# Bias matmuls of batch 0 on four quarter tiles, and one transpose of batch 2 moved from DMA to PE, in a fused attention and token-mixing kernel

## The chip, the cores and the metric

The kernel runs on one core of one Trainium2 chip. The metric is the device time of one execution in microseconds, lower is better. A core has five engines with an instruction queue each: PE (TensorE, matrix products), DVE (VectorE), ACT (ScalarE), POOL (GpSimd) and SP (SyncE, here only an issuer of DMAs). Two on-chip memories matter: SBUF, 128 partitions wide, which all engines and the DMA engines reach, and PSUM, into which PE writes its products and from which DVE and ACT read. One PSUM bank holds 512 float32 numbers per partition.

## What is computed

Attention with a window and a few global keys, and then a token-mixing layer on its output, for 4 batches of 768 tokens, 8 heads of 64 channels:

```python
# attention; n_global = 8, n_local = 96
scores = scale * np.matmul(q, k.transpose(0, 1, 3, 2))
rel = pos[:, None] - pos[None, :]
is_global = pos[None, :] < int(n_global)
is_local = (rel >= 0) & (rel < int(n_local))
keep = is_global | is_local
dist = np.where(is_global & ~is_local, float(n_local), np.abs(rel))
slopes = 2.0 ** (-8.0 * (np.arange(H) + 1) / H)
scores = np.where(keep, scores - slopes[:, None, None] * dist, -1e9)
attn = softmax(scores) @ v                    # to x: 4 x 768 x 512
# mixing
theta = x @ w_theta
zr, zi = x * cos(theta), x * sin(theta)
u = x + w_tok_r @ zr + w_tok_i @ zi           # over tokens
out = u + relu(u @ w_ch)
```

The inputs are float32; the kernel casts them to bfloat16 on load and accumulates in float32.

## The kernel before, in words

**Tiles.** The 768 tokens are 6 tiles of 128 (`NT`), the 8 heads 4 pairs (`NP`); a pair's two heads lie in partitions 0 to 63 and 64 to 127 of `qT` and `kT` (channels in the partitions). Scores are made transposed, keys in the partitions, queries along the row: a key tile meets its own query tile and the next one, and through `kG`, a copy of a key tile whose first 8 keys are replaced by the global keys, the same matmul serves the window and the global keys. A *chunk* is two key tiles (`c` = 0, 1, 2), up to 4 blocks of 128 columns for each of two heads, one PSUM bank for each head: tile `pb`, 128 x 2 x 512. There are two such buffers.

**Biases.** The distances with their mask are a small table, `dist` (128 x 6 blocks x 128, `distances`, L121). In batches 1 to 3 the bias is multiplied in after the exponential, as a table `etab` (L322, L325 on DVE). In batch 0 it is added in PSUM by PE: `score_bias` (L278) multiplies a diagonal matrix `diag[:, h]`, which holds the head's slope, with the distances (L283, one matmul for each head, 512 columns, 384 in chunk 2), and `score_mms` (L287) accumulates the scores on it (L303, contraction over 64 channels in one half of the rows). `score_exp` (L309) is ACT's exponential (L313).

**Values and x.** `values` (L346) multiplies with v and a column of ones (L362); DVE takes the reciprocal (L371) and writes the normalized output to `x_sb` (L373). `vglob` (L335, L343 and L344 on DVE) makes `vG`, the v tiles with the global rows. `xtrans` (L375) turns a pair's part of x into `xT`, channels in the partitions: through a DMA transpose on SP (L377), or through six PE transposes against the identity (L384) into a small PSUM tile and a copy (L385). Batch 0 and pair 3 of batch 1 take the PE way, all others the DMA.

**Mixing.** `theta` (L390) multiplies `xT` with `w_theta` (L405), chunk by chunk of two token tiles; its first step leaves out the last quarter of the contraction, which is pair 3, and does it last. `sines` (L410) makes cos and sin on ACT (L415) and the products `zri` on DVE (L419). `mix` (L424) is the token mixing (L430), with `u` on DVE (L435); `utrans` (L439) turns `u`, by DMA (L444) or by PE (L448); `chan` (L451) is the last product (L458), the ReLU and sum on DVE (L463) and the output DMA on SP (L465). Small PSUM tiles (`ps`) come from a pool of four, in turn.

**Order.** Batch 0's attention and the start of its mixing are ordered by hand (L530 to L619), on all five queues. After that each batch's mixing is woven with the next batch's attention by weights (`weave`, L514, with the steps from `attention_steps`, L485), and a scheduler places what the queues run. POOL issues the loads, casting on the way (L73, L82, L88, L154, L158, L163): those of batch 0 and the weights at once, the rest as buffers come free. SP issues DMA transposes and outputs.

Of the kernel before, what the change touches and what calls it, by code (L numbers as in the profile page):

```python
# [10 lines left out]
BF = mybir.dt.bfloat16  # L11
# [5 lines left out]
def kernel(  # L17
# [13 lines left out]
    nc = tc.nc  # L31
    B, H, S, D = q.shape
    T = 128
# [3 lines left out]
    NP = H // 2  # L37
# [8 lines left out]
    const = ctx.enter_context(tc.tile_pool(name="const", bufs=1))  # L46
# [6 lines left out]
    def ps_big():  # L53
        return big.tile([T, 2, 512], FP, name="pb", tag="pb")

    def ps_small(shape, dtype):
        return small.tile(shape, dtype, name="ps", tag="ps")
# [40 lines left out]
    for i_, eng in ((1, nc.sync), (0, nc.scalar)):  # L98
        eng.dma_start(out=qk32[:, i_].rearrange("p h t d -> p h (t d)"),
                      in_=(q, k)[i_][0, 0:2].rearrange("h (p t) d -> p h (t d)", p=T))  # L100
# [17 lines left out]
    dist = const.tile([T, 6, T], BF)  # L118
    far = const.tile([T, 2 * T], FP)

    def distances():  # L121
        nc.vector.tensor_scalar(far, near, float(NL), 1e6, op0=ALU.is_ge, op1=ALU.mult)
        nc.vector.scalar_tensor_tensor(near, in0=near, scalar=-1e6, in1=near,
                                       op0=ALU.mult, op1=ALU.max)
        d2 = dist[:, 2:4].rearrange("p s n -> p (s n)")
        nc.vector.tensor_tensor(d2, near, far, op=ALU.max)
        nc.vector.memset(dist[0:NG, 3], float(NL))
        nc.vector.tensor_copy(out=dist[:, 0:2], in_=dist[:, 2:4])
        nc.vector.tensor_copy(out=dist[:, 4:6], in_=dist[:, 2:4])
        nc.vector.tensor_scalar(dist[0:NG, 0], dist[0:NG, 2], float(NL), None, op0=ALU.min)  # L130

    diag = const.tile([T, H, T], BF)

    def diagonals(p):
        for h in (2 * p, 2 * p + 1):
            nc.vector.tensor_scalar(diag[:, h], ident, -slopes[h] / scale, None, op0=ALU.mult)
# [41 lines left out]
    def warm(n):  # L178
        ps = ps_small([T, 512], FP)
        for _ in range(n):  # L180
            nc.tensor.matmul(ps, lhsT=zero[:, 0:T], rhs=zero, start=True, stop=True)
# [96 lines left out]
    def score_bias(p, c):  # L278
        pb = pbs[0, p, c] = ps_big()
        n = min(4, 2 * NT - 1 - 4 * c)  # L280
        s0 = 2 if c else 0
        for hh in range(2):
            nc.tensor.matmul(pb[:, hh, 0:n * T], lhsT=diag[:, 2 * p + hh],  # L283
                             rhs=dist[:, s0:s0 + n].rearrange("p s n -> p (s n)"),
                             start=True, stop=False)

    def score_mms(b, p, c):  # L287
        qT, kT, kG = qkT[(b, p)]
# [84 lines left out]
        nc.vector.tensor_mul(xv, po4[:, :, :, 0:D], rec.to_broadcast([T, n, nt, D]))  # L373

    def xtrans(b, p, copy=nc.vector.tensor_copy, i0=0, i1=NT):  # L375
        if b > 1 or (b and p < 3):
            anchor["sp"] = nc.sync.dma_start_transpose(  # L377
                out=xT_sb[b][:, p, :].rearrange("p (t s) -> p t s", t=NT),
                in_=x_sb[b][:, p].rearrange("p t d -> p (t d)")).ins
            return  # L380
        ps = ps_small([T, S], BF)
        own = slice(i0 * T, i1 * T)
        for st in range(i0, i1):
            nc.tensor.transpose(ps[:, st * T:(st + 1) * T], x_sb[b][:, p, st, :], ident)  # L384
        copy(out=xT_sb[b][:, p, own], in_=ps[:, own])  # L385
# [99 lines left out]
    def attention_steps(b, preps):  # L485

        steps = []
        add = lambda w, f, *a: steps.append((w, lambda: f(*a)))
        add(0, alloc_x, b)
        late = [lambda p=p: prep(2, p) for p in range(NP // 2, NP)] if b == 2 else []  # L490
        chunks = [(p, c) for p in range(NP) for c in range(NT // 2)]
        ahead = [preps[:1], preps[1:2], preps[2:]] if preps else [[]] * 3
        if b == B - 1:
            add(0, kglob, b, 0)
        for i_ in range(0, len(chunks), 2):
            steps.append((1800, lambda i_=i_: [scores(b, *pc) for pc in chunks[i_:i_ + 2]]))
            if i_ == 0:
                add(0, vglob, b, 0, H)
            if b == B - 1 and i_ in (0, 2, 6):
                add(0, kglob, b, (1, 2, 0, 3)[i_ // 2])  # L500
            if i_ in (0, 2):
                steps.extend((1536, f) for f in late[i_ // 2:i_ // 2 + 1])
            if i_ == 8:
                steps.extend((1536, f) for f in ahead[0])
            for p in [p for p in range(NP) if (i_ // 2, p) in ((2, 0), (3, 1), (5, 2))]:
                add(1600, lambda p=p: [values(b, p, 0), values(b, p, 1)])
                add(800, xtrans, b, p, nc.scalar.copy)
        steps.extend((1536, f) for f in ahead[1])
        add(1600, lambda: [values(b, NP - 1, 0), values(b, NP - 1, 1)])
        add(800, xtrans, b, NP - 1, nc.scalar.copy)  # L510
        steps.extend((1536, f) for f in ahead[2])
        return steps
# [21 lines left out]
    dve, act = nc.vector.tensor_copy, nc.scalar.copy  # L534
    warm(6)
    distances()
    diagonals(0)
    score_bias(0, 0)
    score_bias(0, 1)
    cast0(1, dve, 0)  # L540
    bias_table(0)
# [19 lines left out]
    for p in range(NP - 1):  # L561
        score_exp(0, p, 1)
        out0(p + 1, 1, act)
        out0(p + 1, 0, dve)
        kglob(0, p + 1)
        score_bias(p, 2)
        score_mms(0, p, 2)
        if p:
            values(0, p - 1, 0)
            values(0, p - 1, 1)  # L570
        score_exp(0, p, 2)
        if p < 2:
            vglob(0, 4 * p, 4)
        score_bias(p + 1, 0)
        score_mms(0, p + 1, 0)
        if p + 2 < NP:
            turn0(p + 2, 1)
            turn0(p + 2, 0)
        score_exp(0, p + 1, 0)
        score_bias(p + 1, 1)  # L580
        score_mms(0, p + 1, 1)
        if p == 1:
            xtrans(0, 0)
    p = NP - 1
# [121 lines left out]
```

## Time and profile before

| what | value |
|---|---|
| median of 4 runs | 172.67 us (172.3 to 173.05) |
| the profiled execution's own time | 172.3 us |
| its span, first to last instruction | 170.5 us |
| PE busy, instructions | 158.5 us, 1516 |
| DVE busy, instructions | 125.4 us, 267 |
| ACT busy, instructions | 100.8 us, 129 |
| L283, bias matmuls: 24 issued, 21 records | 0.38 us each in the median, with their latency |
| L377, DMA transposes of x: 11 | 3.1 us from issue to landing in the median |
| granted PE clock | full throughout |

The profile is of one execution. Busy time of PE includes a matmul's latency, so that pipelined matmuls overlap in it; how often PE takes a new one is read from the distance between starts. The chain of waits follows the work that ended last back to what released it; idle time of an engine off this chain costs nothing. A few matmul records are missing from the trace.

### The profile page before, as it was taken

The page shows a single profiled execution, that of the slowest core. Times are in us where ns is not written, and L with a number is a line of the kernel's source. Part 1 is how long each engine was busy: PE and PEld are TensorE (multiplying, and loading weights), DVE is VectorE, ACT ScalarE, POOL GpSimd, SP SyncE. Part 2 cuts the span into 40 slices and gives each one's busy share as a digit, 9 for nine tenths or more (in the row PEclk, how much of TensorE's full clock was granted, in tenths as well). Part 3 has the DMA queues.
Part 4 walks back from the last instruction along what each step waited for, and adds up shares of the span by engine and source line. Part 5 has one row for each costly group of instructions (what it writes and reads, how often), then busy time and mean ns, then how long its engine had stood idle before and what let it go on. Part 6 is the DMA issues. An engine that isn't in the chain of part 4 may idle for free.

```text
span 170.5 us, 3718 instructions
## 1 busy us (share of the span) xinstructions
PE 158.5 (93%) x1516; PEld 84.6 (50%) x1540; DVE 125.4 (74%) x267; ACT 100.8 (59%) x129; POOL 37.9 (22%) x45
## 2 busy tenths in 40 slices
PE   7679898999999999999999999999999999999991
PEld 2355564555656456444555464444554644444440
DVE  6636786498999999977898788688776856614432
ACT  4698767998488568399954560799348309400010
POOL 8966238001374120299000000000000000000000
PEclk9999999999999999999999999999999999999999
DMA  4999999999999999899999669779135472323335
GB/s 142 200 172 177 207 212 203 204 208 182 151 204 185 185 146 186 123 129 197 153 109 112 140 154 135 173 141 261 35 77 138 98 177 75 117 57 97 95 92 185
DMA packets 74288, 25.73 MB, mean 151 GB/s; under 512 B 62368, under 2 KB 71328, under 8 KB 74272
## 3 DMA queue, kind: packets, MB, share of 16 engines
q0 software_dynamic: 45680, 12.45, 78.2%
q1 hardware_dynamic: 28176, 12.52, 33.8%
q10 hardware_dynamic: 416, 0.52, 0.9%
q8 instruction: 12, 0.20, 0.5%
q14 instruction: 4, 0.03, 0.1%
HBM read 25.69 MB, written 6.29 MB: 188 GB/s over the span
## 4 chain that ended last, share of the span: by engine, by line
PE 62%; DVE 19%; DMA 9%; POOL 4%; ACT 4%; issue 1%; DVEq 0%; POOLq 0%
PE ps L430 30%; PE ps L458 9%; PE pb L405 7%; DMA vn<-in_v_dram 7%; PE pb L303 4%; PE ps L405 4%; PE pb L362 3%; DVE qT L257 3%; POOL qk L73 3%; DVE x_sb L373 2%; DVE e L322 2%; DMA xT<-x_sb 2%; DVE e L325 1%; DVE o_sb L463 1%; ACT cs L415 1%
## 5 line engine op out<-in xcount | busy, mean ns | idle before, releaser
L430 PE MATMUL ps<-zri,w_tokT 128*128 128x512 bf16 x273 | 67.7, 380 | 1.1 <-issue 0.3
L313 ACT ACTIVATE e<-pb 128x1024 bf16<-128x1024 f32 (+1 forms) x48 | 43.7, 954 | 19.1 <-PE pb L303 18.6
L430 PEld LDWEIGHTS <-w_tokT 128*128 128x128 bf16 x288 | 25.9, 98 | 28.0 <-DVE w_tokT L175 0.6
L435 DVE TENSOR_TENSOR u<-x_sb,ps 128x512 bf16<-128x512 bf16 x24 | 16.3, 680 | 11.0 <-PE ps L430 10.9
L458 PE MATMUL ps<-w_ch_bf,uT 128*128 128x512 bf16 (+1 forms) x97 | 24.2, 371 | 0.2
L419 DVE TENSOR_TENSOR zri<-x_sb,cs 128x1024 bf16<-128x1024 bf16 (+1 forms) x30 | 16.6, 581 | 5.9 <-ACT cs L415 5.9
L463 DVE SCALAR_TENSOR_TENSOR o_sb<-ps,u 128x512 f32<-128x512 f32 (+1 forms) x25 | 16.4, 663 | 4.1 <-PE ps L458 3.6
L415 ACT ACTIVATE cs<-pb,halfpi 128x1024 bf16<-128x1024 f32 x8 | 8.9, 1114 | 15.9 <-PE pb L405 15.9
L303 PE MATMUL pb<-qT,kT 64*128 64x128 bf16 x224 | 15.4, 219 | 2.4 <-DVE qT L218 1.4
L322 DVE TENSOR_TENSOR e<-e,etab 128x1024 bf16<-128x1024 bf16 (+1 forms) x24 | 14.8, 618 | 3.1 <-ACT e L313 3.0
L303 PEld LDWEIGHTS <-kT 64*128 64x128 bf16 x224 | 8.9, 94 | 14.9 <-issue 12.0
L405 PE MATMUL pb<-w_theta_bf,xT 128*128 128x512 bf16 x61 | 15.0, 379 | 0.7 <-DVE xT L385 0.3
L362 PEld LDWEIGHTS <-e 128*128 128x128 bf16 x352 | 12.9, 97 | 4.6 <-issue 2.2
L449 ACT COPY uT<-ps 128x512 bf16<-128x512 bf16 x7 | 4.2, 594 | 18.2 <-PE ps L448 18.2
L405 PEld LDWEIGHTS <-xT 128*128 128x128 bf16 x96 | 9.0, 98 | 11.3 <-DMA xT<-x_sb 1.2
L458 PEld LDWEIGHTS <-uT 128*128 128x128 bf16 x100 | 9.1, 98 | 9.6 <-ACT uT L449 0.8
L88 POOL DMA_DIRECT2D vn<-in_v_dram x5 | 9.6, 1928 | 14.3 <-DVE qkn L238 12.6
L303 PE MATMUL pb<-qT,kG 64*128 64x128 bf16 x128 | 11.5, 216 | 0.7 <-DVE kG L229 0.4
L373 DVE TENSOR_TENSOR x_sb<-pb,rec 128x768 bf16<-128x768 f32 x12 | 11.4, 953 | 0.3
L362 PE MATMUL pb<-vn,e 128*128 128x65 bf16 x168 | 9.7, 193 | 0.5 <-DVE x_sb L373 0.3
L325 DVE TENSOR_TENSOR e<-e,etab 128x1024 bf16<-128x1024 bf16 x12 | 8.2, 687 | 2.4 <-ACT e L313 2.4
L259 ACT COPY kT<-ps 128x768 bf16<-128x768 bf16 x8 | 6.4, 797 | 4.6 <-PE ps L253 4.4
(76 smaller groups left out, 204.1 us busy)
## 6 DMA issues: line engine op xcount, KB each, us to landing
out_dram<-o_sb SPq DMA_DIRECT2D x23, 256.0 KB, 2.4
vn<-in_v_dram POOLq DMA_DIRECT2D x3, 768.0 KB, 20.2
qk<-in_q_dram POOLq DMA_DIRECT2D x2, 768.0 KB, 20.9
qk<-in_k_dram POOLq DMA_DIRECT2D x2, 768.0 KB, 23.8
w_nat<-in_moe_w_tok_r_dram POOLq DMA_DIRECT2D x3, 384.0 KB, 15.5
w_nat<-in_moe_w_tok_i_dram POOLq DMA_DIRECT2D x3, 384.0 KB, 14.7
vn<-in_v_dram POOLq DMA_DIRECT2D x2, 384.0 KB, 10.3
qk<-in_q_dram POOLq DMA_DIRECT2D x8, 96.0 KB, 9.0
```

The source lines that it names most:

```text
L303: nc.tensor.matmul(pb[:, hh, o:o + T], lhsT=lhsT, rhs=qT[R, (own, nxt)[part]], start=bool(b), stop=bool(b) or (jt == NT - 1 or (j == 1 and ...
L313: ins = nc.scalar.activation(e_c, pb[:, :, 0:n], AF.Exp, scale=scale).ins
L322: nc.vector.tensor_mul(e_c, e_c, tab[:, :, s0:s0 + n // T].rearrange("p a s n -> p a (s n)"))
L362: nc.tensor.matmul(o, lhsT=l_, rhs=r_, start=(i_ == 0), stop=(i_ == len(mms) - 1))
L373: nc.vector.tensor_mul(xv, po4[:, :, :, 0:D], rec.to_broadcast([T, n, nt, D]))
L405: nc.tensor.matmul(pb[j_] if last else pb[:, j_, :], lhsT=xT[:, dc, st(j_)], rhs=w_theta_bf[:, dc, :], start=(dc == 0), stop=(dc == NC - 1))
L415: nc.scalar.activation(o, p_, AF.Sin, **bias)
L419: anchor["zri"] = nc.vector.tensor_mul(zri[b][:, i_, 2 * c + j_:2 * c + j_ + n, :].rearrange("p j (g d) -> p j g d", g=NP), xb[:, :, 2 * c ...
L430: anchor["pe"] = nc.tensor.matmul(ps, lhsT=w_tokT[wi][:, st, tt * T:(tt + 1) * T], rhs=zri[b][:, wi, st, :], start=(st == 0 and wi == 0), ...
L435: anchor["dve"] = nc.vector.tensor_add(u_sb[b, tt].rearrange("p (g d) -> p g d", g=NP), x_sb[b][:, :, tt, :], ps.rearrange("p (g d) -> p g ...
L458: nc.tensor.matmul(ps_c, lhsT=uT[:, dc, :], rhs=w_ch_bf[:, dc, i_ * n:(i_ + 1) * n], start=(dc == 0), stop=(dc == NC - 1))
L463: nc.vector.scalar_tensor_tensor(o_sb[:, cols], in0=ps_c, scalar=0.0, in1=u[:, cols], op0=ALU.max, op1=ALU.add)
```

## The change

Two edits. First, a copy `distS` of the distance table with its two partition halves exchanged is made by two DMAs on SP, right after `distances()`. In `score_bias`, all pieces except chunks 0 and 1 of pair 0 then issue four matmuls of 64 rows by 64 columns in place of two of 128 by 128. Since the left-hand matrix is diagonal, each of its two nonzero 64 x 64 blocks is enough for half of the output: head 0 uses the two diagonal quarters of the array with `dist`; head 1 uses the two other quarters, with `distS`, so that the rows of distance of keys 64 to 127 enter through partitions 0 to 63, and the other way round. The same sums come out. Second, `xtrans` of pair 3 of batch 2 takes the PE way, with the copy on ACT, as that of batch 1 did.

```diff
+    half = T // 2
+    distS = const.tile([T, 6, T], BF)
+
+    def swap_distances():
+        nc.sync.dma_start(out=distS[0:half], in_=dist[half:T])
+        nc.sync.dma_start(out=distS[half:T], in_=dist[0:half])
+
     diag = const.tile([T, H, T], BF)
...
         pb = pbs[0, p, c] = ps_big()
         n = min(4, 2 * NT - 1 - 4 * c)
         s0 = 2 if c else 0
+        if p == 0 and c < 2:
+            for hh in range(2):
+                nc.tensor.matmul(pb[:, hh, 0:n * T], lhsT=diag[:, 2 * p + hh],
+                                 rhs=dist[:, s0:s0 + n].rearrange("p s n -> p (s n)"),
+                                 start=True, stop=False)
+            return
         for hh in range(2):
-            nc.tensor.matmul(pb[:, hh, 0:n * T], lhsT=diag[:, 2 * p + hh],
-                             rhs=dist[:, s0:s0 + n].rearrange("p s n -> p (s n)"),
-                             start=True, stop=False)
+            for r in range(2):
+                K, M = slice(r * half, (r + 1) * half), slice((r ^ hh) * half, ((r ^ hh) + 1) * half)
+                nc.tensor.matmul(pb[M, hh, 0:n * T], lhsT=diag[K, 2 * p + hh, K],
+                                 rhs=(distS if hh else dist)[K, s0:s0 + n].rearrange("p s n -> p (s n)"),
+                                 start=True, stop=False)
...
     def xtrans(b, p, copy=nc.vector.tensor_copy, i0=0, i1=NT):
-        if b > 1 or (b and p < 3):
+        if b > 2 or (b and p < NP - 1):
             anchor["sp"] = nc.sync.dma_start_transpose(
...
     warm(6)
     distances()
+    swap_distances()
     diagonals(0)
```

In the built program the order of the instructions on each engine is otherwise the same: 20 more matmuls (L283) and 6 more (L384) on PE, one copy more on ACT (L385), two DMAs more and one DMA transpose fewer on SP.

## The prediction, made before the result was known

> **What bounds the kernel now.** I read the page first, then the chain of waits in order of time, then each engine's timeline around the two places that the diff touches.
>
> ```profile
> span 170.5 us, 3718 instructions
> ...
> PE 158.5 (93%) x1516; PEld 84.6 (50%) x1540; DVE 125.4 (74%) x267; ACT 100.8 (59%) x129; POOL 37.9 (22%) x45
> ```
>
> PE is the fullest engine, but 93% is an average, so each edit has to be placed on the chain. For the biases the stretch is 0 to 30 us (columns: start, length, what):
>
> ```profile
> 7.14 11.60 DMA vn<-in_v_dram
> ...
> 18.76 0.44 DVE vG L343
> ...
> 20.11 0.86 DVE qT L218
> ...
> 21.21 0.43 DVE kG L229
> ...
> 21.70 0.23 PE pb L303 x2
> 21.93 0.54 PE pb L283 x2
> 22.47 0.33 PE pb L303 x8
> ...
> 23.91 0.32 PE pb L283 x2
> ```
>
> Until 18.76 us the chain is not PE: it is the second load of v for batch 0, queued behind everything that POOL issued before it. DVE, which had finished at 17.79, waits for it:
>
> ```profile
> 18.76 0.43 DVE L343 COPY vG<-vn 128x1040 bf16<-128x1040 bf16 x1 [0.97 <-DMA vn<-in_v_dram]
> ```
>
> Then DVE runs without a hole to 21.64 (v's copy, xT, qT and kG of pair 3), and PE's scores of pair 3 wait for that kG. From 21.70 to 42 us the chain is PE's, with short pieces of ACT and DVE (exp at 24.55, x_sb at 28.57) that themselves wait for PE's scores and values. So a bias matmul (L283) that is issued before 21.70 shortens work that ends in a wait, and one after it shortens the chain. Two of the ten changed pieces lie after it: (pair 3, chunk 1), 512 columns a head, and (pair 3, chunk 2), 384.
>
> For x of batch 2 the chain reads:
>
> ```profile
> 102.78 0.94 PE ps L430 x5
> 103.72 3.13 DMA xT<-x_sb
> 106.85 0.05 issue
> 106.90 2.33 PE pb L405 x10
> ```
>
> The DMA transpose holds 3.13 us of the chain, but that is not what PE loses, since PE does other work during it:
>
> ```profile
> 104.34 1.03 PE L458 MATMUL ps<-w_ch_bf,uT 128*128 128x512 bf16 x4
> 105.20 1.46 PE L405 MATMUL pb<-w_theta_bf,xT 128*128 128x512 bf16 x5
> 106.90 2.33 PE L405 MATMUL pb<-w_theta_bf,xT 128*128 128x512 bf16 x10 [0.24 <-DMA xT<-x_sb]
> ```
>
> The first theta step issues six matmuls that don't need pair 3 (three dc for two tiles; one record is missing). At 0.216 each (four L458 take 0.86 from 104.34 to 105.20) they are issued by 106.50. The next starts at 106.90: the hole is 0.40 us.
>
> **The change, part by part.**
>
> *The half-swapped copy.* Two DMAs on SP, each 64 rows of 1,536 bytes, 196.6 KB together. SP has nothing queued between its load of k at 0.74 us and an output at 58 us, so nothing waits behind them there. They wait for the last write of dist, which ends at 3.64. SP's load of k took 4.4 us from issue to landing, an output takes 2.4: so they land between about 6.1 and 8.6. The first reader is the bias of (0, 2) at 9.86: hidden, with at least 1.2 us of cover; if it were later, PE would stall there and the 0.97 us of slack at v would take that up first. What isn't hidden is the time on the DMA engines (last two columns: DMA share, GB/s):
>
> ```profile
> 3.00:4.50 1.50, 1.50 (x5) 0.33 (x4) 0.70 (x5) 0.74 (x1) 1.50 (x3) 1.00 1.00 365
> ...
> 13.50:18.50 5.00, 4.67 (x87) 2.81 (x87) 3.27 (x9) 3.57 (x6) 2.56 (x3) 1.00 1.85 183
> ```
>
> The DMA engines are full without a break until v lands, and v is queued behind what they serve; 183 GB/s are bf16 bytes written, twice as many f32 bytes are read. The nearest row for the copy is 3.0 to 4.5 us, when mostly the two f32 loads with 1,536-byte rows move: 365 GB/s, so 196.6 KB cost 0.54 us. Below: 0, if the loads wait on HBM's side and a copy inside SBUF fits beside them. The Trainium skill ("DMA: Bandwidth & Descriptors", Issuing engines are not separate DMA queues) speaks against that: transfers from different engines end up on the same 16 DMA engines. I take +0.50 us on v's landing, 0 to +0.8; from there it goes one to one through DVE to PE at 21.70.
>
> *Biases on quarter tiles.* Each 128-row matmul per head becomes two of 64 by 64, so a piece has four matmuls on four different quarters of the array. Does the trace show such sharing? Two kinds, each with two tiles:
>
> ```profile
> 12.37 0.86 PE L207 MATMUL ps<-ident,qk 128*64 128x128 bf16 x24
> 13.17 0.60 PE L283 MATMUL pb<-dist,diag 128*128 128x512 bf16 x2
> 13.71 0.23 PE L303 MATMUL pb<-qT,kT 64*128 64x128 bf16 x2
> ```
>
> The 24 transposes on column halves are issued in 0.80 us, 33 ns each, where a full-width one takes 57 ns (six L384 from 23.08 to 23.41, 0.33); row halves (L303) run 14 in 0.50 us on the chain, 36 ns each. So halves do run two at a time. A bias piece now takes 0.53 us of PE (21.87 to 22.40): two streams of 0.216 and about 0.10 of changing over. If all four quarters run together, one stream remains: −0.216 us for 512 columns and −0.162 for 384. But four weight loads now stand where two stood; at the 33 ns a piece of the column halves, the last of four starts 0.10 late. So −0.12 to −0.216 and −0.06 to −0.162. A changeover before and after the piece exists already, since scores (row halves) stand on both sides.
>
> Here a rule speaks against the change. "TensorEngine Tiling (Array Packing)", Gotcha 1, says: "Different row tiles cannot access same PSUM bank simultaneously". The two matmuls of one head are different row tiles and write one bank, to different partition halves, and they are issued next to each other. In the trace the row halves of L303 write different banks and the column halves of L207 have the same rows, so no row decides it. By the rule, first and second run one after the other, third beside second at best, so three streams stand where two did: +0.216 and +0.162, and at worst all four in a row, twice that. By the rows the two pieces give −0.18 to −0.38. I take the rows, −0.26 for the two, because the outputs are in disjoint partitions, and keep +0.38 (+0.76) as a rival.
>
> The other eight pieces cost or save nothing at the end: their gain, about 0.1 to 0.2 each, ends in the wait at 18.76 or, for (3, 0) at 20.50, in the waits for qT and kG at 21.03 and 21.70. If v landed before 17.79 that cover would be gone and some three pieces, one per round of the PE to ACT to PE loop, would count too: up to −0.6.
>
> *x of pair 3 of batch 2 on PE.* Removed: one DMA transpose and the 0.40 us hole. Added: six transposes, a PSUM slot and one ACT copy. The build's order puts the six after the third mix matmul behind the chan at 101.75, thus at 103.26. They need the x_sb of this row:
>
> ```profile
> 102.22 0.96 DVE L373 TENSOR_TENSOR x_sb<-pb,rec 128x768 bf16<-128x768 f32 x1
> ```
>
> It ends at 103.18, and batch 1's transposes start 0.06 us after their x_sb (69.78 to 69.84): so PE waits at most 0.02. Queued behind them are five mix matmuls, a chan and theta. The price is 0.34 (69.84 to 70.18, where the next group starts) to 0.36. Their PSUM slot was last read by the u add of 100.98, so it is free. The ACT copy took 0.80 in batch 1; ACT is idle from 100.85 to 107.54, and it also waits for the DMA of pair 2, issued at 101.10 and still the last wait at 105.48. So xT is there by about 106.3 and theta asks for it at 106.50 + 0.36 = 106.86: covered by half a us; were it not, the old hole would come back on top. Net −0.40 + 0.36 = −0.04.
>
> On SP the removal frees 1.3 us in a run of transposes issued back to back from 101 to 116 us, so uT of tile 5 and the kT/qT of pairs 1 to 3 of batch 3 go out that much earlier. DVE waits 0.42 for such a kT at 115.52, but PE at 116.27 waits for ACT's exp, whose chain (sines from 107.54, table load, exp at 115.19) starts with theta. I give this 0, with −0.2 as its far end.
>
> **The sum.** +0.50 − 0.26 − 0.04 = +0.20 us. The profiled execution took 172.30 us (span 170.5 and 1.8 around it), so it would be 172.5; the median of the runs is 172.67, 0.37 above, and the same difference gives 172.87.
>
> **The rivals.**
> *One bank, one row tile (slower).* Batch 0's bias matmuls serialize: 0.50 + 0.38 − 0.04 = +0.84, 173.5; with all four in a row +1.22, 173.9. For: the rule above. Against: disjoint partitions. It decides as soon as a 512-column piece takes over 0.53 us on PE; from 0.73 on the result is slower by over 0.3%.
> *The copy is free (faster side).* v lands at 18.7 as before: −0.26 to −0.38 and −0.04 to −0.24: 172.1 to 172.4. Only if v also ceases to bind, with the 0.6 above, does it pass 0.3%: about 171.9. For: q0 moves steady rates that HBM may set. Against: the full DMA rows.
> *The transposes do nothing.* Six transposes fill just the hole they remove; this is inside the forecast. It turns slower only if xT comes later than 106.86: each 0.1 is 0.1.
> *The copy costs more than its bytes* (1 us, +0.7, 173.4): if two more active rings slow the loads, as between 8 and 12 us, where they ran at 168 GB/s.
>
> **How the numbers follow.** Runs of before spread from 172.3 to 173.05, so 0.3% (0.52 us: 172.15 to 173.19) is about what a measurement can tell from no change. Forecast case 0.52 (its own range 172.45 to 173.15). Serialized bank 0.16, dear copy 0.12, late xT or another new wait 0.08: slower, 0.36 together, of which 0.03 end within the bound. Free copy 0.12: faster past the bound in most of it, with v no longer binding, 0.11. So faster 0.11, same 0.56, slower 0.33. Range 172.1 (free copy) to 173.6 (serialized bank).
>
> **What would show it.** v's second load lands near 19.2 with DVE's wait there 1.4 us or more (step copy right; 18.7 wrong). The bias rows of (3, 1) span 0.32 to 0.41 us to the next L303 (0.53 or more: quarters don't share). The ten theta matmuls start without a wait for xT, with six L384 near 103.7. The prediction is wrong if PE after 21.7 isn't moved by v, or if a wait for distS appears at 9.9.

## The result, and the profile after

The changed kernel takes 173.28 us in the median (172.57 to 174.58), beside 172.79 for the kernel before. The ratio is 1.0031, with a 95% interval of 1.0021 to 1.0041: +0.54 us, slower by just over 0.3%. Differences in microseconds below are (ratio - 1) x 172.8, so that all refer to the same kernel before. Runs with a mean granted PE clock below 0.993 are slower by 0.2 us in both kernels, and the difference stands without them: 173.18 us on average in 21 runs of the changed kernel, 172.72 in 94 of the kernel before. The profiled execution took 172.72 us, with a span of 170.6. Like the profiled one of before, it lies some 0.5 us below its median, so one trace against one trace does not show the difference; the places do.

The page of the changed kernel, its head and its first part:

```profile
span 170.6 us, 3778 instructions
...
PE 159.5 (94%) x1545; PEld 85.6 (50%) x1566; DVE 125.9 (74%) x267; ACT 101.6 (60%) x130; POOL 37.8 (22%) x45
```

No engine's load changed much, as the counts of the change say. The chain of waits of the changed kernel in batch 0 (start, length, what; L298 is the old L283, L318 the old L303):

```profile
7.13 11.67 DMA vn<-in_v_dram
18.82 0.45 DVE vG L358
...
20.18 0.86 DVE qT L225
21.05 0.21 DVE kG L234
21.28 0.35 DVE kG L236
21.69 0.23 PE pb L318 x2
21.92 0.34 PE pb L298 x4
22.26 0.33 PE pb L318 x8
...
23.84 0.29 PE pb L298 x4
```

The chain is the same one. Its bias rows are shorter, 0.34 where 0.54 stood and 0.29 where 0.32 stood. PE's timeline shows why:

```profile
21.85 0.40 PE L298 MATMUL pb<-dist,diag 64*64 64x512 bf16 x2
21.85 0.40 PE L298 MATMUL pb<-distS,diag 64*64 64x512 bf16 x2
22.19 0.23 PE L318 MATMUL pb<-qT,kT 64*128 64x128 bf16 x2
```

All four matmuls of the piece start at 21.85 and the next kind is taken 0.34 us later, where before it was 0.53. One stream of 512 columns is 0.216 us, two in a row would be 0.43: so the quarters run together, also the two that write one bank (one head's, into different partition halves). The 384-column piece takes 0.29 (23.77 to 24.06) instead of 0.42.

In batch 2 the chain reads:

```profile
102.97 0.65 PE ps L445 x3
103.61 0.34 PE ps L399 x6
103.95 1.08 PE ps L445 x5
...
105.89 3.45 PE pb L420 x16
```

The six transposes (L399) cost 0.34, and theta (L420) is one row of 16 matmuls without a hole. From the start of this mix row to theta's end it is 6.37 us (102.97 to 109.34) against 6.45 before (102.78 to 109.23).

The copy's two DMAs are issued at 3.37 and 3.96 us and land 6.6 and 6.2 us later, near 10. The first reader starts at 10.36, so nothing of the forecast cover is left. v's second load has to be read from several traces, since its landing scatters: DVE's `vG` copy starts at 17.87 to 18.99 in nine traces without the copy (mean 18.40), and at 18.82, 19.00, 19.15 and 19.64 in four with it (mean 19.15). In some of them DVE itself was the last; the landing of v alone is at 17.26 to 18.97 without the copy (mean 18.18) and at 18.80 to 19.62 with it (mean 19.13).

### The profile page after: what moved, and what is told of

Read it like the earlier page. It is cut to its first block, busy times and chain, and to the rows that moved or that the text cites. A ratio compares the mean times of both kernels' runs of the same rounds, so it can differ in the third digit from the quotient of the medians.

```text
span 170.6 us, 3778 instructions
## 1 busy us (share of the span) xinstructions
PE 159.5 (94%) x1545; PEld 85.6 (50%) x1566; DVE 125.9 (74%) x267; ACT 101.6 (60%) x130; POOL 37.8 (22%) x45
## 4 chain that ended last, share of the span: by engine, by line
PE 63%; DVE 17%; DMA 9%; POOL 4%; ACT 4%; issue 1%; DVEq 0%; POOLq 0%
PE ps L445 30%; PE ps L473 9%; PE pb L420 8%; DMA vn<-in_v_dram 7%; PE pb L318 4%; PE ps L420 4%; PE pb L377 3%; DVE qT L264 3%; POOL qk L73 3%; DVE e L337 2%; DMA xT<-x_sb 2%; DVE x_sb L388 2%; DVE e L340 1%; ACT cs L430 1%; DVE qkn L245 1%
## 5 line engine op out<-in xcount | busy, mean ns | idle before, releaser
L328 ACT ACTIVATE e<-pb 128x1024 bf16<-128x1024 f32 (+1 forms) x48 | 43.7, 954 | 19.2 <-PE pb L318 18.9
L318 PE MATMUL pb<-qT,kT 64*128 64x128 bf16 x224 | 15.8, 224 | 1.9 <-DVE qT L225 1.3
L337 DVE TENSOR_TENSOR e<-e,etab 128x1024 bf16<-128x1024 bf16 (+1 forms) x24 | 14.7, 617 | 3.1 <-ACT e L328 3.0
L318 PEld LDWEIGHTS <-kT 64*128 64x128 bf16 x224 | 9.2, 95 | 13.8 <-issue 11.7
L420 PE MATMUL pb<-w_theta_bf,xT 128*128 128x512 bf16 x62 | 14.9, 379 | 0.4 <-DVE xT L400 0.3
L420 PEld LDWEIGHTS <-xT 128*128 128x128 bf16 x96 | 9.1, 98 | 11.1 <-DMA xT<-x_sb 0.7
L318 PE MATMUL pb<-qT,kG 64*128 64x128 bf16 x128 | 11.8, 221 | 0.9 <-DVE rec L386 0.8
## 6 DMA issues: line engine op xcount, KB each, us to landing
vn<-in_v_dram POOLq DMA_DIRECT2D x2, 384.0 KB, 10.8
```

The source lines that it names most:

```text
L318: nc.tensor.matmul(pb[:, hh, o:o + T], lhsT=lhsT, rhs=qT[R, (own, nxt)[part]], start=bool(b), stop=bool(b) or (jt == NT - 1 or (j == 1 and ...
L328: ins = nc.scalar.activation(e_c, pb[:, :, 0:n], AF.Exp, scale=scale).ins
L337: nc.vector.tensor_mul(e_c, e_c, tab[:, :, s0:s0 + n // T].rearrange("p a s n -> p a (s n)"))
L420: nc.tensor.matmul(pb[j_] if last else pb[:, j_, :], lhsT=xT[:, dc, st(j_)], rhs=w_theta_bf[:, dc, :], start=(dc == 0), stop=(dc == NC - 1))
```

## The experiments

A table of what each variant does to the time. "Quarters" are the four-quarter biases, "copy" is the half-swapped table made by DMA, "x" is the second edit.

| variant | quarters | copy | x on PE | ratio to before, 95% interval | us |
|---|---|---|---|---|---|
| the change | yes | yes | yes | 1.0031 [1.0021, 1.0041] | +0.54 |
| e_x | | | yes | 0.9994 [0.9979, 1.0009] | -0.10 |
| e_q | yes | yes | | 1.0073 [1.0048, 1.0099] | +1.26 |
| e_copy | | yes | | 1.0043 [1.0027, 1.0059] | +0.74 |
| e_copy2 | | twice | | 1.0122 [1.0099, 1.0146] | +2.11 |
| e_nocopy | yes | | | 1.0024 [1.0010, 1.0038] | +0.41 |
| e_nocopy_x | yes | | yes | 0.9979 [0.9964, 0.9994] | -0.36 |
| e_pe | yes | by PE | yes | 0.9984 [0.9971, 0.9998] | -0.28 |

Where lines of the traces are compared, the starts of the `u` adds on DVE (24 in all) serve as milestones, in us:

| `u` add | before | after | after again | e_copy | e_copy2 | e_nocopy | e_nocopy_x | e_pe |
|---|---|---|---|---|---|---|---|---|
| first (batch 0) | 39.50 | 39.39 | 39.47 | 39.86 | 41.00 | 38.51 | 39.01 | 39.46 |
| 6th (batch 0's end) | 69.70 | 69.67 | 69.61 | 70.13 | 71.22 | 68.68 | 69.15 | 69.68 |
| 7th | 83.22 | 83.41 | 84.06 | 84.07 | 85.23 | 82.97 | 83.46 | 83.28 |
| 11th | 100.98 | 101.17 | 101.83 | 101.84 | 102.99 | 100.73 | 101.22 | 101.05 |
| 12th | 104.54 | 105.06 | 105.72 | 105.39 | 106.55 | 104.29 | 105.12 | 104.95 |
| 13th | 115.97 | 116.08 | 116.74 | 117.04 | 118.32 | 116.57 | 116.14 | 115.97 |
| 24th (last) | 163.95 | 164.07 | 164.71 | 165.06 | 166.31 | 164.55 | 164.12 | 163.95 |

In all the traces but that of e_x12, three stretches hardly vary: 30.1 to 30.4 us from the first to the sixth, 17.76 or 17.77 from the seventh to the eleventh, 47.97 to 48.02 from the thirteenth to the last. What differs is when the first one comes, which v's landing sets for the most part, the stretch from the sixth to the seventh (13.5 to 14.5) and the one from the eleventh to the thirteenth (14.7 to 15.8, and 18.6 in e_nocopy_act).

### The parts one by one

The second edit alone (e_x):

```diff
-        if b > 1 or (b and p < 3):
+        if b > 2 or (b and p < NP - 1):
             anchor["sp"] = nc.sync.dma_start_transpose(
```

> The kernel before with the second edit alone (x of pair 3 of batch 2 on PE; biases as before, no copy). Theory A (the loss is the copy's): the transposes fill the hole they remove, -0.04 to -0.1 us, so 172.5 to 172.8 beside a before of 172.7. Rival B (the loss comes from the transposes or the shifted SP queue): +0.3 to +0.6 us, about 173.2.

Measured: -0.10 us, with zero inside the interval, as forecast.

The first edit alone (e_q), which is the change with the condition of `xtrans` left as it was:

> The first edit alone (quarter tiles with the half-swapped copy; pair 3 of batch 2 by DMA as before). Theory A: all of the loss is here, +0.5 to +0.6 us against before, about 173.3. Rival B: within 0.2 us of before.

Measured: +1.26 us, more than either theory expected. The edits do not seem to add up: with the first in place, the second is worth -0.72 us (from +1.26 to +0.54, give or take 0.5), without it -0.10 (give or take 0.3). PE's timeline of e_q shows the stall that the forecast's "if it were later" spoke of:

```profile
9.77 0.35 PE L298 MATMUL pb<-dist,diag 64*64 64x384 bf16 x2
9.85 0.32 PE L298 MATMUL pb<-distS,diag 64*64 64x384 bf16 x1
10.63 0.32 PE L298 MATMUL pb<-distS,diag 64*64 64x384 bf16 x1 [0.46 <-DMA distS<-dist]
```

The second half of the swapped table lands after it is asked for. DVE still waits for v at 19.64, for 1.74 us, so v's wait takes this stall up.

The copying DMAs alone, read by nothing (e_copy):

```diff
+    half = T // 2
+    distS = const.tile([T, 6, T], BF)
+
+    def swap_distances():
+        nc.sync.dma_start(out=distS[0:half], in_=dist[half:T])
+        nc.sync.dma_start(out=distS[half:T], in_=dist[0:half])
...
     distances()
+    swap_distances()
```

> The kernel before with the two copying DMAs alone: the half-swapped table is made and nothing reads it; biases and transposes as before. Theory A (the copy's DMA time delays the loads behind it): +0.5 to +0.9 us, at least as slow as the whole change, since no bias gets shorter. Rival C (PE's wait for the copy, or the quarter tiles themselves, cost the time): within 0.2 us of before.

Measured: +0.74 us (0.47 to 1.02), for two transfers that nobody reads or waits for. DVE's timeline, at v's second load:

```profile
19.15 0.43 DVE L350 COPY vG<-vn 128x1040 bf16<-128x1040 bf16 x1 [0.83 <-DMA vn<-in_v_dram]
```

The copy made twice (e_copy2) doubles the suspected cost:

```diff
         nc.sync.dma_start(out=distS[0:half], in_=dist[half:T])
         nc.sync.dma_start(out=distS[half:T], in_=dist[0:half])
+        nc.sync.dma_start(out=distS[0:half], in_=dist[half:T])
+        nc.sync.dma_start(out=distS[half:T], in_=dist[0:half])
```

> The kernel before with the copy made twice, one after the other into the same tile, read by nothing. Theory A (DMA time ahead of a full queue): about twice what one copy cost, +1.2 to +1.7 us; v's second load lands 1 us later than with none. Rival (a fixed cost of having the two DMAs, or of the order on SP): about the same +0.7 us as one copy.

Measured: +2.11 us (1.71 to 2.52), above the 1.7 expected. The second pair is issued at 10.0 and 10.8 us, when the first has landed. The same line of DVE's timeline:

```profile
20.44 0.43 DVE L352 COPY vG<-vn 128x1040 bf16<-128x1040 bf16 x1 [1.60 <-DMA vn<-in_v_dram]
```

v is 2.0 us later than the mean without a copy, and the table of milestones shows the first `u` add 1.50 us later than before and the last 2.36. That the copy delays v, and that v's delay reaches the end, is shown by the dose; its price is more than the 0.54 us that its bytes make. The surplus is there when v lands: v's copy on DVE starts 0.75 us later on average with one copy and 2.0 with two, and the times are 0.74 and 2.11 longer. The doubling adds transfers as well as bytes, so it doesn't tell which of the two is paid for.

The quarters without the copy (e_nocopy): head 1's quarters read `dist` itself, so head 1's biases are other numbers, while every instruction on PE is the same. The copy's two DMAs are gone, and the condition of `xtrans` is the old one:

```diff
...
-                                 rhs=(distS if hh else dist)[K, s0:s0 + n].rearrange("p s n -> p (s n)"),
+                                 rhs=dist[K, s0:s0 + n].rearrange("p s n -> p (s n)"),
...
```

> Quarter tiles without the copy: head 1 of each pair reads the distance table itself in place of its half-swapped copy, so its biases in batch 0 are those of the other key half; no copying DMA, transposes as before. Theory A: faster than before by the two bias pieces after v's landing, -0.1 to -0.35 us. Rival C (the tiles themselves lose): +0.2 us or more. In the profile the four matmuls of pair 3, chunk 1 should take about 0.34 us to the next scores.

Measured: +0.41 us. This was the clearest miss. The first 69 us go better than expected: at the sixth `u` add the kernel is 1.02 us ahead. Most of that is luck of this execution: v's copy starts at 17.87 instead of 18.76, which makes 0.89 of it. At the seventh it is 0.25 ahead, at the thirteenth 0.60 behind. The chain of waits of e_nocopy names the first place:

```profile
65.87 0.86 DVE x_sb L383
66.73 0.03 DVE kG L229
66.76 4.20 DMA xT<-x_sb
...
71.00 0.39 PE pb L415
```

Theta of batch 1 waits for the DMA transpose of x of pair 2, which takes 4.20 us here. In the kernel before, theta's first row stands behind PE's own work (the x_sb of 68.81, six transposes, `chan`):

```profile
69.84 0.51 PE ps L384 x6
...
70.57 0.86 PE ps L458 x4
71.43 0.22 PE pb L405
```

A lead from batch 0 ends in this wait. In the eight traces whose chain goes through this transpose it takes 3.65 to 4.35 us, and the stretch from the sixth to the seventh `u` add is 10.1 us longer than it every time; in the six others that stretch is 13.05 to 13.75. The second place is the one that the second edit removes. PE's timeline of e_nocopy:

```profile
104.95 1.46 PE L415 MATMUL pb<-w_theta_bf,xT 128*128 128x512 bf16 x5
107.50 2.33 PE L415 MATMUL pb<-w_theta_bf,xT 128*128 128x512 bf16 x10 [1.09 <-DMA xT<-x_sb]
```

From the first theta row to the second it is 2.55 us, where before it was 1.70 (105.20 to 106.90). SP's queue shows why, in e_nocopy:

```profile
100.84 1.22 SPq L387 DMA_TRANSPOSE xT<-x_sb  x1
102.16 2.45 SPq L454 DMA_TRANSPOSE uT<-u  x1
104.71 1.24 SPq L387 DMA_TRANSPOSE xT<-x_sb  x1
```

and in the kernel before:

```profile
101.10 1.22 SPq L377 DMA_TRANSPOSE xT<-x_sb  x1
102.42 1.21 SPq L444 DMA_TRANSPOSE uT<-u  x1
103.72 1.60 SPq L377 DMA_TRANSPOSE xT<-x_sb  x1
```

The issue of uT took 2.45 us instead of 1.21, so x of pair 3 went out at 104.71 instead of 103.72. In this trace the hole accounts for the loss: 0.25 ahead less 0.85 is the 0.60 behind that stays to the end.

Both without the copy (e_nocopy_x), to see whether the second edit cures this:

> Quarter tiles without the copy (head 1 reads the distance table itself, so its biases in batch 0 are those of the other key half) and x of pair 3 of batch 2 on PE. Theory D: the second edit removes the transpose that was delayed, so -0.1 to -0.4 us against before. Rival E: +0.2 us or more, as without the second edit.

Measured: -0.36 us, as theory D expected. So the second edit is worth -0.77 us on the quarters without the copy (give or take 0.35), as it was -0.72 on those with it, and the copy costs +0.74 alone, +0.85 on the quarters (1.26 - 0.41, give or take 0.5) and +0.90 on both (0.54 + 0.36, give or take 0.3).

The traces show where the second edit earns this. From the eleventh to the thirteenth `u` add it is 14.91 or 14.92 us in all six with the second edit. Without it, it is 14.99 before, 15.54 in e_q and 15.84 in e_nocopy; 15.20 to 15.40 in e_copy, e_copy2 and e_shift, which have no quarters; and 14.70 in e_nocopy_shift. So the edit removes a loss that comes and goes, and not with the quarters alone.

### Why the two edits hang together

What lengthens that issue of uT? The page lists a DMA queue of kind "instruction" (q8, 12 packets, 0.20 MB), and in the traces one of its packets arrives just when the lengthened transpose is issued: at 102.03 us in e_nocopy, where before it came at 103.28. That these packets are PE's instructions is a reading: forty PE instructions more (20 quarter matmuls with their weight loads) come with a packet about 1 us earlier. In the 14 traces, 44 transposes took more than 1.5 us to issue on SP, and a packet of q8 fell on every one of them; the 397 on which none fell took 1.5 at most. Many with a packet took 1.2 all the same. To test whether the place of the packets makes the loss, twenty matmuls of one column were put into the warm-up of the kernel before (e_shift):

```diff
+        for _ in range(20):
+            nc.tensor.matmul(ps[:, 0:1], lhsT=zero[:, 0:T], rhs=zero[:, 0:1], start=True, stop=True)
```

> The kernel before with 20 matmuls of one column added to the warm-up of PE (40 PE instructions, as many as the quarter tiles add), nothing else changed. Theory D (a fetch of PE's instructions comes 1 us earlier at 102 us, meets the DMA transpose of uT on SP and delays the one of x of pair 3): +0.4 to +0.6 us, with an SP entry near 102 us that takes 2 us instead of 1.2, and theta waiting 1 us or more for xT. Rival E (the quarter tiles themselves cost the time): within 0.2 us of before.

Measured: 1.0002 [0.9985, 1.0020], no difference, where theory D expected +0.4 to +0.6. The trace shows the coincidence (the packet of q8 comes at 101.68): SP's queue in e_shift has

```profile
101.96 2.00 SPq L446 DMA_TRANSPOSE uT<-u  x1
104.06 1.24 SPq L379 DMA_TRANSPOSE xT<-x_sb  x1
```

and its theta rows stand 2.11 us apart (104.75 to 106.86) instead of 1.70. So the issue and the hole are longer with the instructions shifted, but the 0.4 us is not seen in the medians. And in the changed kernel uT's issue is lengthened as well (1.94 us at 102.60) without harm: x of pair 3 no longer stands behind it.

The other way round, forty instructions more in the quarters without the copy, so that the packet is moved further (e_nocopy_shift; the same two lines on top of e_nocopy):

> Quarter tiles without the copy (head 1 reads the distance table itself, so its biases in batch 0 are those of the other key half), x of pair 3 by DMA as before, and 20 matmuls of one column in the warm-up, so that PE's instruction fetch of 102 us comes about 1 us earlier still. Theory D (the fetch's meeting with the transpose of uT delays the one of x): the loss of the quarter tiles without copy, +0.41 us, shrinks to within 0.2 us of before or a gain, and the SP entry of 2 us or more stands elsewhere than on the uT just ahead of x of pair 3. Rival: +0.4 us stays.

Measured: 1.0018 [0.9999, 1.0037], +0.31 us, between the two theories and telling neither apart. In its trace the packet comes at 101.79, uT's issue is back at 1.21 us and theta's 16 matmuls take 3.57 us, 0.1 more than without a hole, but in that execution v's copy started at 18.83 and the lead was never there.

Last, the late transpose was taken out of SP's queue: in e_nocopy_act it is issued by ACT, which is idle there.

```diff
+        if b == 2 and p == 3:
+            nc.scalar.dma_start_transpose(
+                out=xT_sb[b][:, p, :].rearrange("p (t s) -> p t s", t=NT),
+                in_=x_sb[b][:, p].rearrange("p t d -> p (t d)"))
+            return
         if b > 1 or (b and p < 3):
```

> The quarter tiles without the copy (head 1's quarters read the unswapped distances, so its biases are not the reference's), x of pair 3 of batch 2 still transposed by DMA, but issued from ACT's queue, which is idle there from 100.6 to 108 us, in place of SP's, where uT of tile 4 held it back to 104.71. Theory A (in the quarter-tile kernel this transpose stands too late in SP's queue, and that is what the second edit takes away): issued at about 103.3, landing 3 us later, so that the ten theta matmuls wait 0.4 us or less instead of 1.09; 172.45 +- 0.2, 0.15% to 0.3% below the kernel before. Theory B (the second edit helps the quarter tiles in another place): the wait may shrink but the median stays at +0.4 us, 173.1 +- 0.2. A hole that is no shorter, since two queues' transposes take turns, would leave A open.

Measured: 1.0137 [1.0087, 1.0187], +2.37 us. The hole grew to 2.25 us, so theory A stays untested. The chain of waits of e_nocopy_act:

```profile
102.18 3.46 DMA uT<-u
105.64 0.02 issue
105.66 0.04 ACTq L387
...
105.82 2.82 DMA xT<-x_sb
108.64 0.05 issue
108.68 3.97 PE pb L420 x10
```

Here ACT's transpose was not begun before SP's had landed: it was issued at 105.82, 0.18 us after uT's landing, and theta starts at 108.68. The run is useful for another reason. The ten theta matmuls take until 112.49, 1.64 us more than the 2.17 of e_nocopy. The windows of e_nocopy_act (busy time and count of each engine, then the granted PE clock, DMA share, GB/s):

```profile
104.10:106.40 2.30, 2.30 (x11) 0.88 (x9) 2.08 (x5) 0.00 (x0) 0.00 (x0) 1.00 0.73 198
106.40:108.70 2.30, 0.05 (x2) 0.02 (x2) 0.70 (x3) 0.00 (x0) 0.00 (x0) 0.98 0.44 86
108.70:110.50 1.80, 1.80 (x5) 0.70 (x6) 0.00 (x0) 0.75 (x1) 0.00 (x0) 0.50 0.34 68
110.50:112.50 2.00, 2.00 (x8) 0.68 (x7) 1.38 (x2) 1.28 (x2) 0.00 (x0) 0.62 0.55 103
112.50:115.00 2.50, 2.50 (x13) 1.17 (x12) 1.46 (x4) 2.03 (x2) 0.00 (x0) 1.00 0.84 157
```

After a hole of 2.2 us PE is granted half its clock for 1.8 us and 0.62 of it over the next 2.0. The span is 2.8 us longer than that of e_nocopy (173.9 against 171.1): 1.18 of later theta and 1.64 of slower matmuls. So lateness in this place reaches the end in full. The trace of e_q has it too (uT's issue 2.11 us, a wait of 0.79 before theta's second row); how often it occurs behind the medians of e_nocopy and e_q is what no run here shows.

### The wait at 71 us

If a lead from batch 0 ends in theta's wait for x of batch 1, moving that transpose to PE as well should let it through (e_x12):

```diff
-        if b > 1 or (b and p < 3):
+        if b > 2 or (b and p < NP - 1 - (b == 1)):
```

> The kernel before with x of pair 3 of batch 2 and x of pair 2 of batch 1 on PE. In the profiles theta of batch 1 waits near 71.4 us for the DMA transpose of pair 2, which shares the DMA engines with the token loads of batch 3. If that wait holds the chain, -0.2 to -0.5 us against before; if PE's six more transposes cost what the wait cost, within 0.2 us of the kernel with pair 3 alone (172.55).

Measured: 1.0039 [1.0022, 1.0055], +0.67 us, worse than either expectation. The chain of e_x12:

```profile
61.97 0.80 ACT kT L259
62.77 0.49 ACT uT L449
63.25 0.94 ACT e L313
...
66.81 0.36 PE ps L384 x6
...
70.94 3.45 PE pb L405 x16
```

Theta has no hole any more (16 matmuls in one row). But the six transposes stand in PE's queue ahead of other work, PE waits for ACT's kT and exp on the way, and from the first to the sixth `u` add it is 31.10 us instead of 30.20. To the seventh it is 13.05 instead of 13.52, so the wait does give way; but then the chain meets a new one, for a DMA transpose of uT that takes 8.30 us (from 83.91), and the last add comes 0.93 later than before. What the wait at 71 us costs is thus not measured by it.

The changed kernel, profiled again beside the last kernels (after_again), shows that place in an unlucky execution:

> The changed kernel once more, for a second profile. In its first profile v's second load landed at 18.80 us, in the two profiles with the copy alone or with quarter tiles at 19.1 and 19.6. Theory A: it lands at 19.0 to 19.7 here, the span is 171.0 to 171.6, and the time stays at +0.4 to +0.7 us against before.

Measured: 1.0051 [1.0029, 1.0073], +0.88 us, above the expected 0.7; the interval takes in that of the first comparison. Span 171.2. PE's timeline:

```profile
72.10 3.19 PE L420 MATMUL pb<-w_theta_bf,xT 128*128 128x512 bf16 x14 [0.75 <-DMA xT<-x_sb]
```

At the sixth `u` add it is 0.09 us ahead of the kernel before, at the seventh 0.84 behind, and it ends 0.76 behind. The same kernel's first profile lost 0.22 between these two. The transpose took 4.35 us here and 3.65 there. So a part of the result is decided at 71 us by how long it takes; what decides that is not shown.

### A version without the copy's price

The swapped table can be made by PE: two matmuls with halves of the identity put the halves of `dist` into the other partitions of a PSUM tile, one DVE cast and one DVE copy bring it to `distS` (the fifth and sixth block equal the third and fourth). Pair 0 keeps full-width matmuls, since the table is ready a little later; the second edit is in (e_pe):

```diff
     def swap_distances():
-        nc.sync.dma_start(out=distS[0:half], in_=dist[half:T])
-        nc.sync.dma_start(out=distS[half:T], in_=dist[0:half])
+        ps = ps_small([T, 4 * T], FP)
+        for r in range(2):
+            nc.tensor.matmul(ps[r * half:(r + 1) * half], lhsT=ident[:, (1 - r) * half:(2 - r) * half],
+                             rhs=dist[:, 0:4].rearrange("p s n -> p (s n)"), start=True, stop=True)
+        nc.vector.tensor_copy(out=distS[:, 0:4], in_=ps.rearrange("p (s n) -> p s n", s=4))
+        nc.vector.tensor_copy(out=distS[:, 4:6], in_=distS[:, 2:4])
...
-        if p == 0 and c < 2:
+        if p == 0:
...
```

> The whole change, with the half-swapped table made by PE in place of the two DMAs (two matmuls against the identity's halves, one copy from PSUM and one inside SBUF on DVE, early in batch 0; pair 0 keeps full-width biases, pairs 1 to 3 use quarter tiles). Theory A (the loss of the change is the copy's DMA time): the copy's cost is gone, -0.1 to -0.5 us against before, like the quarter tiles without a copy and with the second edit. Rival F (v's load binds whatever PE does, so quarter tiles bring nothing): -0.2 to +0.1, like the second edit alone. Rival G (the two copies on DVE delay pair 1): +0.2 or more.

Measured: 0.9984 [0.9971, 0.9998], -0.28 us; the change as made, measured beside it, stood at 1.0051. So the table from PE takes the copy's price away. It has the lowest ratio of the kernels that compute the reference, but less than the 0.3% named above, and its interval overlaps that of the second edit alone (-0.10): that the quarters gain anything beside that edit is not shown by the times. DVE's timeline of e_pe:

```profile
9.38 0.69 DVE L140 CAST distS<-ps 128x512 bf16<-128x512 f32 x1 [1.28 <-PE ps L138]
10.10 0.23 DVE L141 COPY distS<-distS 128x256 bf16<-128x256 bf16 x1
```

These 0.92 us of DVE lie in time that otherwise ends in the wait for v: in this trace DVE is done at 18.86 and v lands at 18.97. Where v lands earlier, as in some other traces, they would count.

## Why the prediction was right or wrong

*The number.* Forecast 172.87 in a range of 172.1 to 173.6; measured 173.28. The likeliest case's own range (172.45 to 173.15) is missed by 0.13, of which 0.12 is the kernel before, 172.79 in more runs instead of 172.67. The sum said +0.20 and +0.54 was measured; the effect lies at the bound of 0.3%, on the slower side, which had 0.33.

*The half-swapped copy, +0.50: the step that failed, by its size.* The mechanism held: the copy delays v, and v's delay goes through DVE to PE. Its size by bytes at 365 GB/s was too small: +0.74, +0.85 and +0.90 us in the three pairs of kernels that differ in the copy alone, and +2.11 for two. Singly the first two leave room for 0.50; the third and the pair of copies don't. The rival "The copy costs more than its bytes" (+0.7, 173.4) is what happened. The landing was mis-sized too: "between about 6.1 and 8.6" became about 10, since a transfer issued by SP beside the full queue took 6.2 to 6.6 us and not 2.4 to 4.4. The 1.2 us of cover were gone, and the wait for distS at 9.9, named as a sign of being wrong, did appear, with 0.46 us in e_q and 0.6 in after_again; it did no harm, since v's wait (1.74 and 1.05 us) came after it, as the forecast had it for that case. The other sign, v near 19.2 with a wait of 1.4, can't be read from one trace: the changed kernel's first has v at 18.80 and a wait of 0.38, since DVE was late itself, its second 18.98 and 1.05. Why the copy costs more than its bytes is not shown; the runs show only how much, and that it is lost by v's landing. (SP's next entry after its load of k is an output at 52.82, not at 58; nothing hangs on it.)

*Quarters, -0.26 for the two pieces.* The rows were the better guide: 0.34 and 0.29 us instead of 0.53 and 0.42, together -0.32, inside the forecast's 0.18 to 0.38. The rule of the Trainium skill ("TensorEngine Tiling (Array Packing)", Gotcha 1) would have made the first piece at least 0.75 (0.53 and one more stream of 0.216); two row tiles that write different partition halves of one bank ran together here, and the measurement decides. The rival "One bank, one row tile" is refuted. But only about half of the -0.32 is on the chain afterwards: the first `u` add of the changed kernel comes 0.11 earlier than before, 0.17 if v's 0.06 is allowed for. From v's copy on DVE to that add it is 20.56 us on average in the eight traces with quarters and 20.72 in the six without. Where the rest went is not shown.

*x of pair 3, -0.04.* Alone it is -0.10 +- 0.26: right, and so were its pieces (0.34 for the six transposes, theta without a wait). What the forecast lacked is that the two edits depend on each other: on the quarters the second is worth -0.72 or -0.77, because without it they lose 0.4 us where they were to gain 0.3. The forecast costed each edit against the kernel before, whose hole of 0.40 is a small one, and gave the freed place on SP's queue 0, with -0.2 as its far end. The change has both edits, so this omission did the number no harm: that is luck. The lateness of that transpose is shown in the traces of e_nocopy and e_q; that the packets of q8 cause it is a coincidence seen in all traces and was not confirmed by the medians.

*The parts together.* Quarters and second edit without the copy: -0.30 forecast, -0.36 measured (give or take 0.26), and -0.28 with the table from PE. The miss, 0.54 - 0.20, is then the copy's: 0.90 in place of 0.50. The rival "The copy is free" (171.9 to 172.4) is refuted by e_copy. "The transposes do nothing" holds for the second edit alone, not beside the first.

*What the forecast left out of its view.* It followed the stretch to 42 us and took the rest as one to one. The milestones show that it isn't: a lead of 1.02 us from batch 0 shrinks to 0.25 in theta's wait at 71 us, while a delay passes, and can grow there (in e_copy from 0.43 to 0.85).

## What to carry to other kernels

Where the DMA engines are full and a load ends the critical wait, price a small transfer placed ahead of it by an experiment that makes it twice, not by its bytes, and ask whether an engine with slack (here PE and DVE) can make the data instead. Two edits far apart in one program can depend on each other through a queue's lateness: measure them alone and together. A gain early in a kernel is worth only what the next fixed arrival leaves of it, so follow it through milestones to the end before it is put into the sum. And read an arrival that scatters from several traces: here one trace would have called the copy free.

## What the runs showed of the hardware

- A hole of 2.2 us on PE (106.44 to 108.68 in e_nocopy_act) was followed by a granted clock of 0.50 and then 0.62 over 3.8 us, which cost another 1.64 us; after the hole of 1.09 us in e_nocopy the clock stayed at 1.00. The Trainium skill ("TensorE: Matmul & The Clock Gate", Part 1: The HAM clock gate) names half clock after an idle window of about 3.4 us; here the shorter hole sufficed, in one trace.
- The granted clock also dipped in the first 20 us of some profiles, with the copy and without (the row for the changed kernel begins 9959999). The 24 transposes at 8.70 then took 1.18 us instead of 0.86; v's wait took this up, 0.38 us of it being left. In the traces of e_x and e_x12, which show the dip too (1.49 and 1.34 us), v had landed at 17.64 and 17.26 and DVE came to it 0.9 us later, so there v's wait didn't.
- The issue of a DMA transpose on SP took 1.2 us as a rule and 1.5 at most when no packet of the queue q8 fell on it (397 in 14 traces); all 44 that took longer, up to 2.5 us, had such a packet with them. In e_nocopy one of 2.45 us put x of pair 3 off by 1 us.
- A DMA transpose issued by ACT waited for SP's to land before it was begun (0.18 us after it). The Trainium skill ("DMA: Bandwidth & Descriptors", Latency and other measured facts) says that two in flight on different queues must be kept apart by software; the trace agrees that they are.
